# A new order of the pieces behind the first 47 in a hand-ordered attention and feed-forward kernel

## Chip, core and metric

The kernel runs on one core of a Trainium2 chip. The metric is the device time of one execution in microseconds (us), the median of the runs. The engines are TensorE (PE; its weight loads are shown as PEld), VectorE (DVE), ScalarE (ACT), GpSimd (POOL) and SyncE (SP), which here only issues transfers.

## What is computed

The reference normalizes x (2048 rows of 512), and adds to x an attention branch A and a feed-forward branch B of the same normalized rows. A has 32 heads of width 16 and walks four segments of 512 rows: causal softmax attention inside a segment, and a linear-attention memory M, z that is carried from one segment to the next and mixed in by a gate per head.

```python
for s in range(N):                      # N = 4 segments
    logits = einsum('bhqd,bhkd->bhqk', qs, ks) * scale + mask
    a_dot = einsum('bhqk,bhkd->bhqd', softmax(logits), vs)
    num = einsum('bhld,bhde->bhle', phi(qs), M)
    den = einsum('bhld,bhd->bhl', phi(qs), z)[..., None] + 1e-06
    outs.append(g * num / den + (1.0 - g) * a_dot)
    M = M + einsum('bhld,bhle->bhde', phi(ks), vs)
    z = z + einsum('bhld->bhd', phi(ks))
out = x + o @ wo + silu(xn @ w1) @ w2   # F = 1792
```

## The kernel before

The whole program is a list of words, ORDER, which is read from left to right; each word calls one small function (a piece), and that call issues its instructions. Every engine executes its own instructions in the order in which they were issued, so the list is the program order of all engines at once. There is no planner in the kernel: the list is written out. A word is a letter code, then the segment, then the tile, then sometimes a part, as in `k0.1.2`: key product, segment 0, tile 1, part 2. A tile is 128 of the 512 columns of q, k (eight heads), 128 rows of v and of the output, or 128 of the 1792 columns of h.

The words that matter here, with the line that their instructions carry in the profile:

- `S0` to `S71`, the scores: products of q and k in a shape of 32 rows (L701) into one tile psS of four PSUM banks, the exponential of all 2048 columns on ScalarE (L707, tile Pb), then two to four causal masks on GpSimd (L718, on Pb or into `lows`). S words are numbered 18 to a segment, nine to a pair of tiles; the list does not have them in the order of their numbers.
- `E`, `O`: the weights times v for the even and the odd heads of a tile (L763, psV), which need the masks of the S words of that tile. `Ev`, `Ov` or `Ea`, `Oa` copy the result out of PSUM on VectorE or ScalarE (L793, L800), and transfers move the sums of the softmax into `zraw` (L785). `Om` merges the odd heads by a predicated copy (L807).
- `k`, `q`, `v`, `h`: products with the weights (L331 as whole 128 x 128 products, L333 as four products 32 columns wide, which run side by side). `kv`, `qv`, `vv` copy them out of PSUM on VectorE, `ka`, `qa`, `va` on ScalarE (L373, L384, L391). A key copy also issues two masks of k on GpSimd (L376), which the scores read.
- `ha`, `hv`: tanh on ScalarE (L477) and the rest of the silu on VectorE (L482).
- `fp`, `fa`, `fv` and `gp`, `ga`, `gv`: phi of k and of q on GpSimd, ScalarE and VectorE (L402, L408, L418). `t` turns phi of k by a transfer (L426).
- `m`, `mv`, `mw`: the sums for the memory on TensorE (L437) and their additions and masks on VectorE. `s`, `sv`, `r`, `w`, `R`, `W`: the sums of the denominators, reciprocals, gate. `z`, `d` spread them by transfers (L562), `zv`, `dv` multiply (L574, L584), `n`, `nv` are the memory's product and its addition (L593).
- `o`, `oc`, `od`, `oh`: output products of a 512-, 256-, 128-column piece, and of half of the last tile; `st`, `sh` add the residual, which `xl` loads (L599), and store (L606, L611, L653, L657).
- `xs`, `xg`, `Nv`, `XD`: layer norm of the later segments (L281, L284, L292, L295, L310) and its turning by transfers (L829). `tb` loads the table for the exponential on ScalarE and runs one small exponential (L304). `lw` issues the loads of w2 and wo from ScalarE's queue.

The products other than the scores, and psV and psM, share four PSUM banks of 512 columns (`pp`, tag "pb"); a word that begins a product takes a free bank and waits for the copy that empties it. The last two output tiles use psS after the last scores.

```python
words = ORDER.split()
TILED = {"S": "rows", "E": "cols", "O": "cols", "s": "cols", "m": "cols", "X": "whole", "busy": "whole"}
...
    elif piece in ("k", "q", "v", "h", "n", "o", "oc", "od", "oh"):
        now = ahead[i] if now == "rows" else now
        now = "whole" if now == "rows" else now
    narrow[0] = now == "cols"
    PIECES[piece](*(int(n) for n in word[len(piece) :].split(".") if n))
```

So a product takes the shape of the words around it, and the shape changes around each S word.

Of the kernel before, what the change touches and what calls it, by code (L numbers as in the profile page):

```python
# [25 lines left out]
S6 vv1.0 v1.1.2 v1.1.3 xs10 lw0 xg8.4 h0.1.3 ha0.1 q1.2.0 t0.0 q1.2.1 q1.2.2 fv0.3 k1.2.0 vv1.1 k1.2.1 k1.2.2 k1.2.3 kv1.2
S8 q1.2.3 fa0.2 h0.2.0 h0.2.1 h0.2.2 h0.2.3 E1 qv1.2 gate hv0.1 h0.7.0
S9 q1.0.0 Ev1 fv0.2 t0.2 k1.1.0 k1.1.1 k1.1.2 Nv10 Nv11 h0.7.1 h0.7.2 h0.7.3 k1.1.3 kv1.1 ha0.7 hv0.7 q1.0.1 q1.0.2 Nv9 ha0.2 hv0.2
S10 h0.4.0 h0.4.1 XD10 t0.1 h0.4.2 h0.4.3 ha0.4 fp1.2 O1 Ov1 hv0.4 q1.0.3 h0.9.0 bmask qv1.0 gp1.0
S13 ga1.0 XD9 k1.3.0 h0.9.1 h0.9.2 k1.3.1 k1.3.2 xl0.2 h0.8.0 h0.8.1 xs13 h0.8.2 h0.8.3 k1.3.3 t0.3 kv1.3 ha0.8  # L30
# [11 lines left out]
S28 h1.4.0 h1.4.1 h1.4.2 q2.3.0 h1.4.3 ha1.4 q2.3.1 qv2.3 o0.0.9
S26 ga2.1 o0.0.1 oc0.0.13.0 od0.0.11.2 oc0.0.4.0 hv1.4 Nv12 O4 Ov4 q2.0.0 zv0.2 q2.0.1 qv2.0 zv0.0
S23 o0.0.2 XD12 h1.1.0 o0.0.16 h1.1.1 h1.1.2 od0.2.0.0 o0.2.16 h1.1.3 xl0.0 h1.12.0 ha1.1 od0.0.11.1 od0.0.11.0
S25 h1.12.1 h1.12.2 Om3 h1.12.3 od0.2.0.1 zv0.3 o0.0.14 oc0.0.4.1 hv1.1 gv1.1 o0.0.17 ha1.12 E5 Ev5 oc0.0.13.1
S29 o0.0.12 hv1.12 o0.0.8 od0.0.11.3 k2.3.0 zv0.1 k2.3.1 fa1.2 O5 kv2.3
S27 h1.6.0 mw0.0 fv1.2 o0.0.10 o0.0.6 t1.2 o0.0.5 gp2.1 h1.6.1 h1.6.2 o0.2.15 Ov5 h1.6.3 ha1.6 o0.0.0 hv1.6
# [5 lines left out]
S34 fp1.1 o0.1.0 v2.0.0 v2.0.1 vv2.0 h1.2.0 h1.2.1 fa2.3 o0.1.16 o0.3.17 Om6
S41 o0.3.8 o0.1.11 o0.1.1 O7 o0.1.14 oc0.1.12.1 fa1.1 o0.3.4 xl1.0 Ov7 o0.1.9
S37 o0.1.2 st0.1 h1.2.2 h1.2.3 o0.3.1 o0.3.3 o0.3.16 xl1.2 ha1.2 o1.2.4 od1.2.5.1 fv1.1 t1.1 m1.2 mv1.2 o1.2.1
S36 s1 hv1.2 o0.3.7 sv1 o0.3.2 fp2.0 r1.0 o0.3.14 st0.3 q3.1.0 q3.1.1 qv3.1 o1.2.12 fp2.3 fa2.0
S40 r1.1 v2.3.0 v2.3.1 vv2.3 h2.8.0 h2.8.1 r1.3 fv2.3 r1.2 ha2.8 hv2.8 q3.2.0
S43 q3.3.0 q3.3.1 qv3.3 w1 o1.2.8 q3.2.1 fa2.2 qv3.2 k3.1.0 d1.1 od1.2.5.2
# [24 lines left out]
S64 o2.0.13 od2.2.6.1 s3 sv3 o2.0.1 h3.12.0 h3.12.1 ha3.12 n2.1 r3.0 nv2.1 o2.2.0
S68 hv3.12 od2.0.7.2 o2.2.17 o2.0.11 h3.2.0 h3.2.1 o2.3.0 r3.2 r3.1 od2.3.9.3 o2.3.1 ha3.2 hv3.2 oc2.3.2.0
# [830 lines left out]
```

## Time and profile before

| what | value |
|---|---|
| median of 3 runs | 222.15 us (222.1 to 222.64) |
| profiled execution | 222.15 us; its span 220.4 us |
| TensorE busy, share of the span | 214.9 us, 97% |
| ScalarE | 184.0 us, 83% |
| VectorE | 179.7 us, 82% |
| GpSimd | 135.1 us, 61% |
| granted TensorE clock | 0.999 |
| S0 on TensorE, S71 on TensorE | 12.51 us, 193.15 us |

The span runs from the first to the last instruction. A timeline row gives the start, the duration, the engine, the line, the operation, output and inputs, shapes, a count where alike instructions stand in a row, and in brackets the idle time before it with what ended it. A group row gives count, busy time and mean duration in ns, then the idle time of the engine before such instructions. A windows row gives, for a stretch of time, busy time and count of each engine in the order PE, PEld, DVE, ACT, POOL, then the granted clock and the transfers' share and rate.

### The profile page before, as it was taken

To read this page: it belongs to the slowest core of one execution; us is meant where nothing else is said; L and a number is where in the kernel's file an instruction comes from. 1 tells how busy PE (TensorE), PEld (TensorE's weight loads), DVE (VectorE), ACT (ScalarE), POOL (GpSimd) and SP (SyncE) were. 2 spreads that over 40 slices of the span, in tenths; PEclk is the share of its full clock that TensorE was granted. 3 is DMA by queue.
4 is the path that set the end of the run, shared out by engine and by line. 5 is a ranking of instruction groups with operands and counts; after the bars stand their busy time and mean duration, and the time that the engine had idled before them with its cause. 6 is when DMAs were issued, how large, how long until landed. Compare 5 with 4: busy or idle time off the path is not lost.

```text
span 220.4 us, 9441 instructions
## 1 busy us (share of the span) xinstructions
PE 214.9 (97%) x4057; PEld 117.2 (53%) x4057; DVE 179.7 (82%) x368; ACT 184.0 (83%) x173; POOL 135.1 (61%) x253
## 2 busy tenths in 40 slices
PE   7999999999999999999999999999999999999994
PEld 7666645655553444454544444455454544455662
DVE  7789999988889788776897888969789887579554
ACT  3699999999999999999998999999989997971000
POOL 6089667997769976876669696693756364320000
PEclk9999999999999999999999999999999999999999
DMA  5993549552014221223303130142242020232313
GB/s 183 373 385 87 74 27 304 106 77 58 21 28 122 88 59 29 50 51 76 102 17 95 40 96 4 28 92 59 52 120 64 15 76 7 75 94 68 109 51 97
DMA packets 32746, 19.61 MB, mean 89 GB/s; under 512 B 14656, under 2 KB 32192, under 8 KB 32704
## 3 DMA queue, kind: packets, MB, share of 16 engines
q1 hardware_dynamic: 30080, 16.39, 28.6%
q10 hardware_dynamic: 2624, 2.62, 3.9%
q8 instruction: 31, 0.51, 1.0%
q14 instruction: 11, 0.09, 0.2%
HBM read 9.96 MB, written 2.10 MB: 55 GB/s over the span
## 4 chain that ended last, share of the span: by engine, by line
PE 79%; ACT 10%; DVE 4%; POOL 4%; issue 2%; POOLq 0%
PE ps L331 21%; PE psO L333 16%; PE ps L333 13%; PE psS L701 10%; PE psO L331 9%; ACT Pb L707 7%; PE psV L763 6%; PE psS L333 4%; POOL Pb L718 2%; DVE xn_t L310 1%; POOL lows L718 1%; ACT ex L408 1%; ACT th L477 1%; PE psM L437 1%; DVE stats L281 1%
## 5 line engine op out<-in xcount | busy, mean ns | idle before, releaser
L707 ACT ACTIVATE Pb<-psS 128x2048 bf16<-128x2048 f32 x72 | 135.2, 1878 | 7.5 <-PE psS L701 6.4
L718 POOL TENSOR_SCALAR_AFFINE_SELECT Pb<-Pb 128x256 bf16<-128x256 bf16 (+2 forms) x120 | 66.1, 571 | 22.3 <-ACT Pb L707 19.5
L482 DVE SCALAR_TENSOR_TENSOR hT<-th,ps 128x512 bf16<-128x512 bf16 x56 | 37.7, 679 | 9.1 <-ACT th L477 8.5
L718 POOL TENSOR_SCALAR_AFFINE_SELECT lows<-Pb 64x256 bf16<-64x256 bf16 (+1 forms) x56 | 26.7, 490 | 27.7 <-ACT Pb L707 25.3
L333 PE MATMUL psO<-w_sb,hT 128*32 128x512 bf16 (+2 forms) x716 | 42.5, 319 | 0.0
L331 PE MATMUL ps<-xnT,w_sb 128*128 128x512 bf16 (+1 forms) x160 | 35.2, 334 | 0.0
L477 ACT ACTIVATE th<-ps 128x512 bf16<-128x512 f32 x56 | 33.0, 598 | 2.2 <-PE ps L333 2.1
L333 PEld LDWEIGHTS <-hT 128*32 128x32 bf16 x884 | 21.8, 96 | 14.0 <-issue 3.3
L333 PE MATMUL ps<-xnT,w_sb 128*32 128x512 bf16 (+1 forms) x480 | 27.1, 341 | 0.1
L701 PE MATMUL psS<-qT,k 32*128 32x64 bf16 (+3 forms) x512 | 23.0, 233 | 0.8 <-ACT Pb L707 0.3
L331 PE MATMUL psO<-w_sb,hT 128*128 128x512 bf16 (+2 forms) x87 | 22.7, 334 | 0.0
L701 PEld LDWEIGHTS <-k 32*128 32x128 bf16 x512 | 9.8, 92 | 23.2 <-issue 21.7
L763 PE MATMUL psV<-Pb,Vz 128*32 128x448 bf16 (+7 forms) x512 | 21.6, 286 | 0.3 <-POOL Pb L718 0.3
L331 PEld LDWEIGHTS <-w_sb 128*128 128x128 bf16 x160 | 14.9, 98 | 12.1 <-issue 1.6
L763 PEld LDWEIGHTS <-Vz 128*32 128x32 bf16 x768 | 16.5, 97 | 9.1 <-issue 1.1
L376 POOL TENSOR_SCALAR k<-kT,pm_odd 128x512 bf16<-128x512 bf16 x16 | 12.0, 748 | 8.0 <-ACT kT L373 7.0
L333 PEld LDWEIGHTS <-w_sb 128*32 128x32 bf16 x480 | 11.9, 96 | 7.3 <-issue 1.9
L331 PE MATMUL ps<-wv_sb,xnT 128*128 128x512 bf16 x56 | 15.1, 381 | 0.2
L701 PE MATMUL psS<-qT,kT 16*128 16x448 bf16 (+3 forms) x256 | 14.7, 269 | 0.0
L333 PE MATMUL psO<-wo_sb,oT 128*32 128x512 bf16 x156 | 14.4, 380 | 0.0
L331 PE MATMUL ps<-xnT,wk_sb 128*128 128x256 bf16 (+1 forms) x64 | 13.6, 326 | 0.0
L793 DVE CAST oraw<-psV 128x512 bf16<-128x512 f32 x16 | 11.0, 689 | 3.0 <-PE psV L763 2.9
(110 smaller groups left out, 321.2 us busy)
## 6 DMA issues: line engine op xcount, KB each, us to landing
spr<-rz SPq DMA_DIRECT2D x56, 64.0 KB
x_res<-in_A_x_dram SPq DMA_DIRECT2D x16, 128.0 KB
out_dram<-o_out SPq DMA_DIRECT2D x15, 128.0 KB
w_sb<-in_B_w_dram SPq DMA_DIRECT2D x1, 1792.0 KB
w_sb<-in_B_w_dram ACTq DMA_DIRECT2D x1, 1792.0 KB
x_hi<-in_A_x_dram SPq DMA_DIRECT2D x2, 512.0 KB
wv_sb<-in_A_wv_dram SPq DMA_DIRECT2D x2, 256.0 KB
wk_sb<-in_A_wk_dram SPq DMA_DIRECT2D x1, 512.0 KB
```

The source lines that it names most:

```text
L281: nc.vector.bn_stats(out=stats[t][:], in_=xs(t, t + 1)[:, 0, :])
L310: eng.tensor_scalar(out=xn[t][:], in0=xs(t, t + 1)[:, 0, :], scalar1=mv_all[:, t, 0:1], scalar2=rstd_all[:, t, 0:1], op0=ALU.subtract, op1 ...
L331: return [nc.tensor.matmul(out, lhsT=lhsT, rhs=rhs, start=start, stop=stop, skip_group_check=True)]
L333: nc.tensor.matmul(out[c : c + 32], lhsT=lhsT[:, c : c + 32], rhs=rhs, start=start, stop=stop, tile_position=(0, c), skip_group_check=True,)
L376: nc.gpsimd.tensor_scalar(out=to, in0=frm, scalar1=keep[:, 0:1], scalar2=1.0, op0=ALU.mult, op1=ALU.mult)
L477: nc.scalar.activation(out=th[:], in_=sts[s]["h", ft][:, :], func=AF.Tanh, scale=0.5)
L482: nc.vector.scalar_tensor_tensor(out=st["hT"][:, ft, :], in0=st.pop(("th", ft))[:], scalar=1.0, in1=st.pop(("h", ft))[:, :], op0=ALU.add, ...
L701: nc.tensor.matmul(psS[:, g, c : c + q2 - q1], lhsT=keys[rows], rhs=st["qT"][rows, dt, q1:q2], start=True, stop=True, tile_position=(32 * ...
L707: exp = nc.scalar.activation(out=Pb[:, :, :], in_=psS[:, :, :], func=AF.Exp, scale=SCALE)
L718: over[id(Pb)].append(nc.gpsimd.affine_select(out=out, in_=in_, compare_op=ALU.is_ge, fill=0.0, base=base, pattern=[[0, out.shape[1]], [1, ...
L763: nc.tensor.matmul(psV[32 * g : 32 * g + 32, q0 : q0 + nq], lhsT=Vzs[s % 2][:, kt, 4 * dt + g, par : par + 2, :].rearrange("p a d -> p (a ...
L793: copy(out=oraw[:], in_=sts[s].pop(("psV", 0))[:, :])
```

## The change

Only ORDER changes. Its first 47 words stay (through `k0.0.1`); the 1286 behind them are in a new order. Both lists have 1333 words. Nine words differ in kind: `qv0.0`, `kv0.1`, `vv2.3`, `Ev14`, `Ev15`, `Oa12` and `Oa14` become `qa0.0`, `ka0.1`, `va2.3`, `Ea14`, `Ea15`, `Ov12` and `Ov14`, and `qa0.1` and `qa3.0` become `qv0.1` and `qv3.0`. The order of the S words among themselves is the same. It is said of the new list that it was searched with the predicated copy at its measured length, and under late small transfers and fetches of instructions.

Behind `k0.0.1` the first line continues:

```diff
-k0.1.0 k0.0.2 k0.0.3 k0.3.0 q0.0.0 q0.0.1 q0.0.2 q0.0.3 ka0.0 fp0.0 qv0.0 tb fa0.0 q0.2.0 k0.1.1 k0.1.2 k0.1.3 kv0.1 fp0.1
+tb xs6 k0.1.0 k0.1.1 k0.0.2 k0.0.3 ka0.0 k0.1.2 fa0.0 q0.0.0 q0.0.1 q0.0.2 q0.0.3 qa0.0 k0.1.3 q0.3.0 q0.3.1 k0.3.0 ka0.1 fp0.1
```

and some whole lines of the list are

```diff
-S0 q0.1.0 q0.1.1 q0.1.2 q0.1.3 k0.3.1 xs4 xs6 xs7 xs5 xg4.4 q0.2.1 q0.2.2 qa0.1 q0.2.3 qv0.2
...
-S1 Nv5 vv0.2 h0.5.0 h0.10.0 h0.10.1 h0.10.2 v0.3.3 vv0.3 xs8 Nv6 XD6 h0.5.1 h0.5.2 XD5 h0.5.3 ha0.5
-S3 q0.3.0 q0.3.1 q0.3.2 q0.3.3 hv0.5 k0.2.0 qv0.3 Nv4 XD4 k0.2.1 k0.2.2 tanh h0.10.3 ha0.10
...
-S15 hv0.12 hv0.9 h1.11.1 h1.11.2 h1.11.3 ha1.11 E2 Ev2 O2 h1.9.0 h1.9.1
...
-S20 z0.2 k2.0.0 hv1.8 z0.1 h1.5.2 h1.5.3 z0.3 gp1.1 k2.0.1 kv2.0 E4 Ev4 ha1.5 hv1.5 od0.2.0.3
...
-S35 od0.1.8.3 o0.1.13 oc0.3.13.0 o0.3.5 o0.3.12 o0.1.7 E7 Ev7 xl0.1 od0.3.10.0 ga1.3 oc0.1.12.0 o0.3.9 gv1.3 fp1.0 fv1.0 t1.0
...
+S0 xs4 k0.3.1 q0.2.0 q0.2.1 xs5 k0.3.2 xs7 v0.2.0 v0.2.1 xg4.4 k0.3.3 fa0.1 q0.3.2 q0.3.3
...
+S1 Nv5 XD5 h0.11.0 hv0.5 fv0.1 h0.11.1 h0.11.2 h0.10.0 h0.10.1 q0.1.1 q0.1.2 h0.11.3 ha0.11 h0.10.2
+S3 Nv4 hv0.11 h0.10.3 ha0.10 q0.1.3 qv0.1 v0.3.0 v0.3.1 v0.3.2 fp0.3 h0.13.0 Nv7 XD7 h0.13.1 h0.13.2 v0.3.3 vv0.3 xs11
...
+S15 E2 Ev2 q1.3.2 q1.3.3 qv1.3 h1.11.1 h1.11.2 gp1.1 h1.11.3 ha1.11 xs12 xs14 xg12.4 o0.2.4
+S17 h1.9.0 h1.9.1 h1.9.2 h1.9.3 ha1.9 h0.0.0 h0.0.1 hv1.11 o0.2.10 XD11 o0.2.1 hv1.9 oc0.2.9.1
+S21 o0.2.12 O2 oc0.2.2.1 oc0.2.9.0 h0.0.2 m0.2 mv0.2 h0.0.3 Ov2 ha0.0 Om2 o0.2.5
...
+S20 k2.0.0 z0.0 h1.5.3 ha1.5 hv1.8 z0.2 z0.3 k2.0.1 kv2.0 oc0.2.2.0 o0.2.7 E4 Ev4 XD14
...
+S34 od0.1.8.2 fv1.3 o0.1.14 t1.3 Om5 o0.1.5 fp1.1 h1.2.0 h1.2.1 h1.2.2 h1.2.3 ha1.2 gv2.1 hv1.2 E7 oc0.3.13.1
```

The last line, behind `S71`, holds the rest of the output products of both lists; it ends in `st3.2` with eight `oh` words and `sh1` in the old list, and in `st3.0` with eight `oh` words and `sh0` in the new one.

More of the change, by code (lines that the diff above doesn't have):

```diff
@@ L26 @@
[L26 to L30, printed above, removed]
@@ L42 @@
[L42 to L47, printed above, removed]
@@ L53 @@
[L53 to L58, printed above, removed]
@@ new lines @@
+kind odd omask ones0 ones1 zeros xc0 xd0 xc1 xq0 xi0 Nv0 busy44 xd1 xq1 xc2 xi1 X0.1 Nv1 xd2 Xa0.1 busy6 v0.0.0 v0.0.1 xq2 X1.1 Xa1.1 xs3 v0.0.2 v0.0.3 xq3 v0.1.0 xi2 v0.1.1 v0.1.2 v0.1.3 Nv2 xi3 X2.1 va0.0 va0.1 Nv3 Xv2.1 X3.1 Xv3.1 k0.0.0 k0.0.1 tb xs6 k0.1.0 k0.1.1 k0.0.2 k0.0.3 ka0.0 k0.1.2 fa0.0 q0.0.0 q0.0.1 q0.0.2 q0.0.3 qa0.0 k0.1.3 q0.3.0 q0.3.1 k0.3.0 ka0.1 fp0.1
+S0 xs4 k0.3.1 q0.2.0 q0.2.1 xs5 k0.3.2 xs7 v0.2.0 v0.2.1 xg4.4 k0.3.3 fa0.1 q0.3.2 q0.3.3
+S2 kv0.3 qv0.3 q0.2.2 q0.2.3 qv0.2 v0.2.2 v0.2.3 vv0.2 q0.1.0 Nv6 h0.5.0 h0.5.1 XD6 h0.5.2 h0.5.3 ha0.5
@@ new lines @@
+S6 h0.2.0 h0.2.1 h0.2.2 Ov0 qv1.0 ga1.1 v1.0.0 fp0.2 v1.0.1 xs13 v1.0.2 v1.0.3 vv1.3 Nv8 XD8 k1.2.0 k1.2.1
+S8 h0.7.0 h0.7.1 Nv10 vv1.0 Nv11 h0.7.2 h0.7.3 h0.2.3 k1.2.2 k1.2.3 kv1.2 ha0.2 hv0.2 ha0.7 hv0.7 E1
+S9 h0.4.0 h0.4.1 h0.4.2 k1.0.0 k1.0.1 h0.4.3 k1.0.2 ha0.4 fv0.0 t0.0 Ev1 O1 Ov1 hv0.4
+S10 Om0 Nv9 XD9 k1.0.3 kv1.0 t0.3 h0.8.0 h0.8.1 h0.8.2 h0.8.3 XD10 q1.2.0 q1.2.1 q1.2.2 q1.2.3 qv1.2 fa0.2 ha0.8 hv0.8
+S13 xs15 h0.9.0 fv0.2 t0.2 k1.1.0 h0.9.1 h0.9.2 h0.9.3 k1.1.1 k1.1.2 k1.1.3 k1.3.0 k1.3.1 ha0.9
@@ new lines @@
+S12 h0.12.0 h0.12.1 h0.12.2 h0.12.3 t0.1 kv1.1 k1.3.2 k1.3.3 hv0.9 q1.3.0 ha0.12 kv1.3 q1.3.1 gate h1.11.0 hv0.12
+S15 E2 Ev2 q1.3.2 q1.3.3 qv1.3 h1.11.1 h1.11.2 gp1.1 h1.11.3 ha1.11 xs12 xs14 xg12.4 o0.2.4
+S17 h1.9.0 h1.9.1 h1.9.2 h1.9.3 ha1.9 h0.0.0 h0.0.1 hv1.11 o0.2.10 XD11 o0.2.1 hv1.9 oc0.2.9.1
+S21 o0.2.12 O2 oc0.2.2.1 oc0.2.9.0 h0.0.2 m0.2 mv0.2 h0.0.3 Ov2 ha0.0 Om2 o0.2.5
+S14 h1.10.0 h1.10.1 h1.10.2 h1.10.3 ha1.10 hv0.0 h0.3.0 h0.3.1 h0.3.2 h0.3.3 gv1.1 m0.0 mv0.0
+S16 hv1.10 od0.2.0.1 lw1 q2.1.0 Om1 q2.1.1 qv2.1 od0.2.0.3 E3 ha0.3 Ev3 o0.2.11 od0.2.0.2 hv0.3 o0.2.13 Nv13
@@ new lines @@
+S19 h0.6.0 h0.6.1 O3 Ov3 h0.6.2 h1.0.0 h0.6.3 ha0.6 h1.0.1 h1.0.2 hv0.6 Nv14
+S24 h1.0.3 k2.2.0 k2.2.1 kv2.2 ha1.0 gp1.0 v2.1.0 v2.1.1 bmask
+S18 o0.2.3 vv2.1 o0.2.8 hv1.0 sv0 v2.2.0 r0.3 r0.0 r0.1 v2.2.1 vv2.2 h1.8.0 ga1.0 h1.8.1 o0.2.6 xl0.2
+S22 h1.8.2 h1.8.3 ha1.8 k2.1.0 r0.2 k2.1.1 h1.5.0 h1.5.1 h1.5.2 kv2.1 w0 z0.1
+S20 k2.0.0 z0.0 h1.5.3 ha1.5 hv1.8 z0.2 z0.3 k2.0.1 kv2.0 oc0.2.2.0 o0.2.7 E4 Ev4 XD14
+S28 xl0.3 hv1.5 q2.3.0 q2.3.1 qv2.3 XD13 h1.4.0 h1.4.1 h1.4.2 h1.4.3 ha1.4 o0.0.9 od0.0.11.3
@@ new lines @@
+S26 q2.0.0 q2.0.1 hv1.4 o0.0.1 zv0.0 fa1.0 qv2.0 O4 Ov4 fp1.3 o0.0.8 oc0.0.4.0
+S23 h1.1.0 oc0.0.13.0 oc0.0.13.1 o0.0.3 Om3 zv0.3 h1.1.1 o0.0.2 h1.1.2 gv1.0 zv0.2 h1.1.3 ha1.1 o0.0.6 hv1.1 gp1.2 h1.12.0
+S25 zv0.1 h1.12.1 h1.12.2 h1.12.3 xl0.0 o0.0.5 o0.0.10 od0.2.0.0 E5 Ev5 o0.0.14 od0.0.11.2 ha1.12
+S29 o0.2.16 hv1.12 ga1.2 o0.0.15 k2.3.0 od0.0.11.1 Nv12 k2.3.1 O5 kv2.3
+S27 h1.13.0 h1.13.1 o0.2.14 Ov5 o0.2.15 gv1.2 o0.2.17 st0.2 h1.13.2 h1.13.3 xl0.1 ha1.13 hv1.13 fp1.0 o0.3.0 od0.3.10.0 od0.3.10.1 od0.3.10.2 fv1.0 oc0.3.11.1
```

95 lines of the change are left out of this document (45 added, 50 removed).

## The prediction

> **What bounds the kernel now.** I read the page first, then the view of waits, then the timeline of TensorE and ScalarE stage by stage; a stage is what lies between two score pieces (S words of the list). The last-ending chain is TensorE's own order nearly throughout, so the question is when TensorE stands still.
>
> ```profile
> PE 214.9 (97%) x4057; PEld 117.2 (53%) x4057; DVE 179.7 (82%) x368; ACT 184.0 (83%) x173; POOL 135.1 (61%) x253
> ```
> ```profile
> PEld L701 <- issue: 21.7, 64, 0.4
> ACT Pb L707 <- PE psS L701: 6.4, 18, 0.7
> PE psV L763 <- POOL Pb L718: 0.3, 1, 0.3
> ```
>
> TensorE waits for other engines hardly anywhere in this view, but that is deceptive: a matmul held back while the one before it drains counts as busy. So I take the distance from score piece to score piece, here the stage of S40 on TensorE:
>
> ```profile
> 108.59 0.21 PE L701 MATMUL psS<-qT,k 32*128 32x64 bf16 x4
> ...
> 108.93 1.04 PE L331 MATMUL ps<-wv_sb,xnT 128*128 128x512 bf16 x4
> 109.80 1.03 PE L331 MATMUL ps<-xnT,w_sb 128*128 128x512 bf16 x4
> 110.66 0.59 PE L331 MATMUL ps<-xnT,wq_sb 128*128 128x512 bf16 x2
> 111.19 0.40 PE L701 MATMUL psS<-qT,k 32*128 32x64 bf16 x8
> ```
>
> Ten products of 512 columns take the stage from 108.59 to 111.19, 2.60 us. Starts 108.93 and 109.80 are four products apart: 0.217 us each, which I call a unit (0.215 below, rounded). The score piece and the change of tile shape around it take the rest, 0.45 us. A stage of u units thus wants 0.45 + 0.215 u. Now a stage with eight units, the one of S3, on TensorE (256-column products, two to a unit) and on ScalarE:
>
> ```profile
> 19.81 0.40 PE L701 MATMUL psS<-qT,k 32*128 32x192 bf16 x8
> 20.14 1.05 PE L331 MATMUL ps<-xnT,wq_sb 128*128 128x256 bf16 x8
> 21.03 0.82 PE L331 MATMUL ps<-xnT,wk_sb 128*128 128x256 bf16 x6
> 21.68 0.38 PE L331 MATMUL ps<-xnT,w_sb 128*128 128x256 bf16 x2
> 22.19 0.21 PE L701 MATMUL psS<-qT,k 32*128 32x64 bf16 x4
> ```
> ```profile
> 17.88 1.88 ACT L707 ACTIVATE Pb<-psS 128x2048 bf16<-128x2048 f32 x1
> ...
> 20.26 1.88 ACT L707 ACTIVATE Pb<-psS 128x2048 bf16<-128x2048 f32 x1
> ...
> 22.64 1.88 ACT L707 ACTIVATE Pb<-psS 128x2048 bf16<-128x2048 f32 x1
> ```
>
> By its units it wants 0.45 + 1.72 = 2.17 us, and it takes 2.38 (19.81 to 22.19), the distance of the exponentials (20.26 to 22.64). There is one score tile in PSUM, so S4 waits for the exponential of S3 (ends 22.14), takes 0.40, and the next exponential starts 0.05 later. That loop is a floor of 2.38 us, or nine units: a stage with fewer loses the difference. So the time is the start of S0, plus 71 stages each the larger of units and floor, plus waits for VectorE and GpSimd, plus the products left behind S71.
>
> ```profile
> 12.51 0.21 PE L701 MATMUL psS<-qT,k 32*128 32x64 bf16 x4
> ...
> 193.15 0.40 PE L701 MATMUL psS<-qT,k 32*128 32x192 bf16 x8
> ...
> 217.16 0.40 PE L333 MATMUL psS<-wo_sb,oT 128*32 128x256 bf16 x8
> ```
>
> S0 stands at 12.51, S71 at 193.15 (71 stages, 180.64 us), the last product ends at 217.56, and the span of 220.4 us leaves 2.87 behind it for the last half tile's addition and store. The profiled execution took 222.15 us, 1.7 outside its span, and is the median of the three times. A difference of 0.3% (0.67 us) is about what a measurement of this kernel can tell from none.
>
> **The change, part by part.** Counted from the lists: both have 1333 words and the same 72 score pieces, so the shape changes cost the same; TensorE has the same products. What moves is which stage a product fills, five PSUM copies between VectorE and ScalarE, and how far a consumer stands behind its producer.
>
> *Start, about +0.4 us.* The exponential table's load (tb) moves ahead of the first key copy (ka0.0); the query copy of tile 0 and the key copy of tile 1 go to ScalarE, ahead of S0's exponential.
>
> ```profile
> 8.93 0.59 ACT L391 CAST Vz<-ps 128x512 bf16<-128x512 f32 x1 [0.19 <-PE ps L331]
> 9.21 1.57 PE L331 MATMUL ps<-xnT,wk_sb 128*128 128x256 bf16 x12
> 10.60 0.59 ACT L373 CAST kT<-ps 128x512 bf16<-128x512 f32 x1 [1.08 <-PE ps L331]
> 11.20 1.28 ACT L304 ACT_TABLE_LOAD   x1
> 12.50 0.20 ACT L304 ACTIVATE spare<-eps 128x1 f32<-128x1 f32 x1
> ```
>
> Before, ScalarE idles from 9.52 to 10.60 and loads behind the copy. After, load and first exponential run 9.52 to about 11.0, so ka0.0 ends at 11.6 instead of 11.19; S0 stood 1.32 behind it (GpSimd's two masks of k), so S0 comes at 12.9: +0.4. The added copies end about when S0's exponential may start. The list now has 15 units between the first key product and S0 instead of 14; by 3.3/14 us each (9.21 to 12.51) these would let S0 start at 12.75, so the bounds are +0.2 and +0.6 (both copies in the way).
>
> *Units moved, -0.55 and +0.3.* From S0 to S71 the old list has 666.75 units, the new 664.25: 2.5 x 0.215 = 0.54 less. Behind S71 there are 111.75 instead of 110.25: 1.5 x 0.215 = 0.32 more. The one unit of difference is the one that now lies before S0.
>
> *Stages below the floor, -0.8.* A sums product of the memory (m) in a stage counts as one unit. The old list has four stages of 8 units (S0, S1, S3, S7), four of 8.5 (S8, S10, S17, S24) and six of 8.75 (S16, S20, S26, S23, S25, S29): 4 x 0.21 + 4 x 0.10 + 6 x 0.05 = 1.54 us lost. The new one has one of 8 (S5), five of 8.5 (S7, S11, S15, S17, S21) and one of 8.75 (S29): 0.76. That is 0.78 less.
>
> *Stages with two small ScalarE pieces, -0.1.* Such a stage has a floor of its own, here the one of S9:
>
> ```profile
> 37.29 1.88 ACT L707 ACTIVATE Pb<-psS 128x2048 bf16<-128x2048 f32 x1
> ...
> 39.06 1.08 ACT L477 ACTIVATE th<-ps 128x512 bf16<-128x512 f32 x2
> ...
> 40.02 1.90 ACT L707 ACTIVATE Pb<-psS 128x2048 bf16<-128x2048 f32 x1
> ```
>
> 2.73 us, the worth of 10.6 units. Twelve become nine; TensorE is often past that anyway, so I take 0.1 and no bound beyond 0.3.
>
> *Waits, -0.45.* Two stages ran long because of GpSimd's masks:
>
> ```profile
> 47.39 0.10 PEld L701 LDWEIGHTS <-k 32*128 32x128 bf16 x4 [0.42 <-issue]
> ...
> 49.58 0.40 PE L763 MATMUL psV<-Pb,Vz 128*32 128x320 bf16 x8 [0.26 <-POOL Pb L718]
> ...
> 50.47 0.40 PE L701 MATMUL psS<-qT,k 32*128 32x192 bf16 x8
> ```
> ```profile
> 96.28 0.40 PE L701 MATMUL psS<-qT,k 32*128 32x192 bf16 x8
> ...
> 96.92 0.44 DVE L807 COPY_PREDICATED oraw<-omask,odd 128x256 int32<-128x256 int32 x1
> 96.96 0.87 POOL L718 TENSOR_SCALAR_AFFINE_SELECT Pb<-Pb 128x512 bf16<-128x512 bf16 x1
> ...
> 98.92 0.40 PE L701 MATMUL psS<-qT,k 32*128 32x64 bf16 x8
> ```
> ```profile
> L718 POOL TENSOR_SCALAR_AFFINE_SELECT Pb<-Pb 128x512 bf16<-128x512 bf16 x48 | 30.9, 661 | 2.2
> ```
>
> S15's stage has ten units (2.60) and takes 3.08: O2 stands one stage behind S12, whose masks are late. S35's has nine (2.38) and takes 2.64: E7 waits for a mask that took 0.87 instead of 0.66, beside a predicated copy. The new list puts O2 two stages later (in S21) and E7 one stage later (end of S34). That takes away 0.48 + 0.26 = 0.74, but it moves other weighings closer (E2 now opens the second stage behind its last mask, and E4 stands 0.3 us earlier behind its own); I keep 0.3 for one new wait of the smaller size. Bounds: -0.74 if none is new, +0.5 if two of O2's size come.
>
> The Trainium skill, SBUF — State Buffer, section "SBUF: two separate sides", says that VectorE with two SBUF inputs and GpSimd share a port pair by an exclusive lock, so that whoever starts second stands still for the whole instruction. The trace agrees, here by 0.21 us (0.87 against 0.66). If each of the two new neighbours of a weighing met such a lock, the sum would be 0.4 higher; without the rule it is the one below.
>
> *Sum:* +0.4 - 0.54 + 0.32 - 0.78 - 0.1 - 0.45 = -1.15 us; 222.15 - 1.15 = 221.0. The end stays as it is: eight half products and one half store behind the last whole tile in both lists, 2.87 us.
>
> **The rivals.** *(1) VectorE falls behind between S0 and S17, slower.*
>
> ```profile
> 12.51:50.47 37.96, 36.97 (x595) 22.11 (x596) 35.48 (x72) 37.33 (x36) 31.54 (x58) 1.00 0.63 140
> ```
> ```profile
> L384 DVE CAST qT<-ps 128x512 bf16<-128x512 f32 x14 | 9.6, 683 | 2.7 <-PE ps L331 2.7
> L281 DVE BATCH_NORM_STATS2 stats<-x_hi 128x6 f32<-128x512 bf16 x8 | 5.4, 673 | 0.0
> L284 DVE BATCH_NORM_AGGREGATE mv_all<-stats 128x2 f32<-128x6 f32 x16 | 2.9, 181 | 0.5
> ```
>
> VectorE (third figure) is busy 35.48 of that stretch's 37.96. The new list puts two more query copies (2 x 0.68) and two more layer-norm sums (2 x 0.85) into it and takes one copy of 0.2 out: +2.86, 38.34 us. If the stretch stays at 37.9 and VectorE idles its old 2.48 in it, it ends 2.9 late, and each late copy holds one of the four PSUM banks that the products share. Against it: the first two sums can run before S0, while VectorE has nothing else (1.7 us of lead), and products wait only once a copy is later than the banks allow. It decides when the lead is lost (VectorE then waits for k0.3's product until S0's stage is over) and the banks cover no more than half a microsecond: then 2.4 reach TensorE, and the time is 223.4.
>
> *(2) The waits come back in other places.* Three waits of the sizes seen (0.48, 0.26 and the 0.21 by which that mask was late) beside the one kept: 221.0 + 0.95 = about 222.0, no change. For it: VectorE, GpSimd and ScalarE all run within a tenth of the stage, so a piece shifted by a few tenths finds no slack.
>
> *(3) The list does not do what it says,* because the floor is not lost where I count it and the copies moved to ScalarE push exponentials back: without the floor's 0.78 the sum is -0.37, 221.8, no change.
>
> **How the numbers follow.** The forecast, about 221.0, has a chance of 0.55; its own range is 220.2 (start +0.2, no new wait, 0.2 more at two-piece stages) to 221.4 (start +0.6, one wait of O2's size more). Rival (2) gets 0.18, rival (3) 0.08, rival (1) 0.19. Range 220.2 to 223.2: above lies part of rival (1), below little. Faster 0.55, same 0.26, slower 0.19.
>
> **What would show it.** Right: S0 near 12.9, the table load at 9.5; S71 near 191.6 (from 12.9 less than 179.0 for 71 stages); the stages of S1 and S3 on nine units at 2.38 with TensorE nowhere short; O2 and E7 without a mask just ended before them; 24.7 us from S71 to the last product. Wrong: products between S9 and S17 that start just as a VectorE copy ends (rival 1), stages of S15, S20, S34 longer than their units because a mask ends late (rival 2), or a start of S0 past 13.3.

## The result: slightly slower

The changed kernel takes 223.07 us (median; 222.44 to 223.84), the kernel before in the same comparison 222.50 (222.07 to 223.66). The ratio is 1.0027, 95% interval 1.0017 to 1.0036: 0.57 us slower, where 221.0 and thus 1.15 us faster was forecast. A second comparison gave 222.94 against 222.32, ratio 1.0031 (1.0016 to 1.0046).

The first profiled execution of the changed kernel took 223.32 us, 0.25 above its median, so a second one (222.78 us) stands beside it. Each span, cut at the places that the prediction used (us):

| kernel | S0 | S0 to S71 | S71 to end of last product | from there to the end | span |
|---|---|---|---|---|---|
| before | 12.51 | 180.64 | 24.41 | 2.87 | 220.4 |
| forecast | 12.9 | 178.8 | 24.7 | 2.87 | 219.3 |
| after | 12.88 | 179.84 | 25.37 | 3.52 | 221.6 |
| after, second profile | 12.82 | 179.93 | 24.73 | 3.49 | 221.0 |

The second profile against before: +0.31 - 0.71 + 0.32 + 0.62 = +0.54 us, which is close to the 0.57 of the medians. The start and the tail's products came as forecast; the stages won 0.7 to 0.8 instead of 1.87; the end, forecast at nothing, lost 0.62.

### The profile page after: what moved, and what is told of

It reads as the page before. It is cut to its first block, busy times and chain, and to the rows that moved or that the text cites. A ratio compares the mean times of both kernels' runs of the same rounds, so it can differ in the third digit from the quotient of the medians.

```text
span 221.6 us, 9593 instructions
## 1 busy us (share of the span) xinstructions
PE 215.4 (97%) x4129; PEld 117.4 (53%) x4129; DVE 179.1 (81%) x367; ACT 185.1 (84%) x174; POOL 136.2 (61%) x253
## 3 DMA queue, kind: packets, MB, share of 16 engines
q1 hardware_dynamic: 30080, 16.39, 27.6%
q10 hardware_dynamic: 2624, 2.62, 3.7%
## 4 chain that ended last, share of the span: by engine, by line
PE 73%; ACT 7%; POOL 6%; DVE 4%; DMA 3%; issue 3%; SPq 2%; DVEq 0%; POOLq 0%
PE ps L331 19%; PE ps L333 14%; PE psO L333 13%; PE psS L701 9%; PE psV L763 7%; PE psO L331 6%; ACT Pb L707 5%; POOL Pb L718 2%; PE psS L836 2%; SPq L562 2%; DMA spr<-rz 2%; POOL k L376 1%; PE psS L333 1%; POOL lows L718 1%; POOL pos L402 1%
## 5 line engine op out<-in xcount | busy, mean ns | idle before, releaser
L718 POOL TENSOR_SCALAR_AFFINE_SELECT Pb<-Pb 128x256 bf16<-128x256 bf16 (+2 forms) x120 | 67.4, 582 | 22.3 <-ACT Pb L707 19.3
L333 PE MATMUL psO<-w_sb,hT 128*32 128x512 bf16 (+2 forms) x744 | 46.5, 323 | 0.0
L331 PE MATMUL ps<-xnT,w_sb 128*128 128x512 bf16 (+1 forms) x156 | 33.2, 332 | 0.1
L333 PE MATMUL ps<-xnT,w_sb 128*32 128x512 bf16 (+1 forms) x496 | 28.1, 344 | 0.0
L331 PEld LDWEIGHTS <-w_sb 128*128 128x128 bf16 x156 | 14.1, 97 | 11.7 <-issue 2.8
L331 PE MATMUL psO<-w_sb,hT 128*128 128x512 bf16 (+2 forms) x80 | 19.3, 327 | 0.1
L333 PEld LDWEIGHTS <-w_sb 128*32 128x32 bf16 x496 | 12.5, 96 | 7.9 <-issue 1.4
L331 PE MATMUL ps<-wv_sb,xnT 128*128 128x512 bf16 x49 | 13.4, 380 | 0.2
L606 DVE SCALAR_TENSOR_TENSOR o_out<-psO,x_res 128x512 bf16<-128x512 f32 x14 | 9.6, 686 | 3.9 <-PE psO L333 2.2
L800 DVE CAST odd<-psV 128x512 bf16<-128x512 f32 x15 | 10.3, 685 | 2.5 <-PE psV L763 2.4
```

Source lines behind the costliest of these rows:

```text
L331: return [nc.tensor.matmul(out, lhsT=lhsT, rhs=rhs, start=start, stop=stop, skip_group_check=True)]
L333: nc.tensor.matmul(out[c : c + 32], lhsT=lhsT[:, c : c + 32], rhs=rhs, start=start, stop=stop, tile_position=(0, c), skip_group_check=True,)
L606: out = nc.vector.scalar_tensor_tensor(out=o_out[:], in0=st.pop(("psO", j)), scalar=0.5, in1=st["x", j][:], op0=ALU.mult, op1=ALU.add)
L718: over[id(Pb)].append(nc.gpsimd.affine_select(out=out, in_=in_, compare_op=ALU.is_ge, fill=0.0, base=base, pattern=[[0, out.shape[1]], [1, ...
L800: copy(out=odd[:], in_=sts[s].pop(("psV", 1))[:, :])
```

## The profile after

The page of the changed kernel, engines and the chain that ended last:

```profile
PE 215.4 (97%) x4129; PEld 117.4 (53%) x4129; DVE 179.1 (81%) x367; ACT 185.1 (84%) x174; POOL 136.2 (61%) x253
...
PE 73%; ACT 7%; POOL 6%; DVE 4%; DMA 3%; issue 3%; SPq 2%; DVEq 0%; POOLq 0%
```

New against before is what stands in the chain beside TensorE: transfers and SyncE's queue, 5% between them. The timeline of the start (ScalarE, then TensorE) and the two score pieces that answer to those quoted before:

```profile
9.59 1.28 ACT L304 ACT_TABLE_LOAD   x1
...
10.99 0.57 ACT L373 CAST kT<-ps 128x512 bf16<-128x512 f32 x1
...
12.88 0.21 PE L701 MATMUL psS<-qT,k 32*128 32x64 bf16 x4 [0.18 <-POOL k L376]
...
192.72 0.40 PE L701 MATMUL psS<-qT,k 32*128 32x192 bf16 x8
```

The table load at 9.59, the key copy to 11.56 and S0 at 12.88 are the forecast's 9.5, 11.6 and 12.9. The two waits that were to go are gone. The stage of S15, now 8.5 units, takes 2.39 (47.38 to 49.77 on TensorE; it was 3.08 with ten units, which want 2.60); the stage of S21, where O2 now stands, takes 2.37 (52.15 to 54.52); that of S35 takes 2.43 (was 2.64).

```profile
47.38 0.21 PE L701 MATMUL psS<-qT,k 32*128 32x64 bf16 x4
...
49.77 0.40 PE L701 MATMUL psS<-qT,k 32*128 32x192 bf16 x8
...
52.15 0.40 PE L701 MATMUL psS<-qT,k 32*128 32x192 bf16 x8
...
54.52 0.21 PE L701 MATMUL psS<-qT,k 32*128 32x64 bf16 x4
```

Others came. The largest three, on the timelines of TensorE, GpSimd and VectorE:

```profile
69.25 0.40 PE L701 MATMUL psS<-qT,k 32*128 32x64 bf16 x8
...
70.99 1.04 PE L763 MATMUL psV<-Pb,Vz 128*32 128x512 bf16 x16
71.96 0.21 PE L701 MATMUL psS<-qT,k 32*128 32x64 bf16 x4
```
```profile
67.99 0.61 POOL L402 TENSOR_SCALAR pos<-qT 128x512 bf16<-128x512 bf16 x1
...
70.59 1.09 POOL L718 TENSOR_SCALAR_AFFINE_SELECT Pb<-Pb 128x1024 bf16<-128x1024 bf16 x1
```
```profile
88.96 0.89 DVE L807 COPY_PREDICATED oraw<-omask,odd 128x256 int32<-128x256 int32 x1
```
```profile
139.81 1.02 PE L331 MATMUL ps<-xnT,wk_sb 128*128 128x512 bf16 x4 [0.19 <-DVE oT L593]
```

In the stage of S20, nine units, E4 takes 1.04 us instead of some 0.72 (what it takes in the last experiment): it stands for the mask that ends at 71.68, which GpSimd reaches late behind the piece of gp1.0 (67.99). The stage takes 2.72 instead of 2.38. In that of S30 (2.62) a predicated copy of 0.89 us (0.44 where it is alone) makes the silu behind it late, whose PSUM bank the next product needs. In that of S51 (2.85, ten units want 2.60) the product k3.3 waits for a bank until the memory's addition (L593) has read it.

And the end, on VectorE and the last product on TensorE:

```profile
211.65 0.42 DVE L574 TENSOR_TENSOR oT<-spr,oraw 128x512 bf16<-128x512 bf16 x1 [1.20 <-DMA spr<-rz]
...
216.19 0.69 DVE L606 SCALAR_TENSOR_TENSOR o_out<-psS,x_res 128x512 bf16<-128x512 f32 x1 [0.82 <-PE psS L333]
216.84 0.42 DVE L653 SCALAR_TENSOR_TENSOR o_half<-psS,x_res 128x256 bf16<-128x256 f32 x1
217.80 0.69 DVE L606 SCALAR_TENSOR_TENSOR o_out<-psO,x_res 128x512 bf16<-128x512 f32 x1 [0.54 <-DMA out_dram<-o_out]
218.78 0.42 DVE L653 SCALAR_TENSOR_TENSOR o_half<-psS,x_res 128x256 bf16<-128x256 f32 x1 [0.28 <-DMA out_dram<-o_out]
```
```profile
212.92 0.29 PE L333 MATMUL psS<-wo_sb,oT 128*32 128x256 bf16 x4 [0.46 <-DVE oT L593]
...
217.81 0.28 PE L333 MATMUL psS<-w_sb,hT 128*32 128x256 bf16 x4
```

The row tiles and the half tiles share three buffers (name "o_out", bufs=3). The new list adds and stores its last five tiles between 214.7 and 219.2, and the last two additions wait, not for TensorE, but for stores issued three before them to land: that is the 3.52 us behind the last product. The row at 211.65 is another matter: the transfer z3.3 lands late and oh17.1 stands at 212.92; in the second profile of the same kernel it does not (below).

## The experiments

Two theories. **E and F**: the loss lies at the end (buffers, E), and in transfers whose last share is held up by a fetch of instructions (F; the page lists 32 of them on a queue of their own, 0.52 MB, so 16 KB each); the stage waits (W) add. **The rivals (N)**: removing any of these only moves the wait. All ratios are to the kernel before, run beside.

**The half stores in other buffers.**

```diff
- o_half = work.tile([P, D], BF16, name="o_half", tag="o_out", bufs=3)[:, 0 : D // 2]
+ o_half = work.tile([P, D], BF16, name="odd")[:, 0 : D // 2]
```

> The changed kernel with one line altered: the two half stores write from the tile "odd" (two buffers, long read out by then) and no longer share the three buffers of the row stores. Nothing of the list is altered. Theory E (the end waits for buffers): sh1, st3.0 and sh0 no longer wait for stores issued three before; last product to end goes back from 3.52 to about 2.9 us, and the kernel takes 0.6 us less, 222.5 against 223.1, level with the kernel before (ratio to it 1.000). Rival N (the end is limited by landing the last stores, whichever buffer they leave from): last product to end stays at 3.4 to 3.5 us and the time at 223.1 (ratio 1.0027).

Measured: 222.33 us, ratio 1.0003 (0.9987 to 1.0019). VectorE's end, and the last product (ends 217.55):

```profile
216.73 0.69 DVE L606 SCALAR_TENSOR_TENSOR o_out<-psO,x_res 128x512 bf16<-128x512 f32 x1
217.60 0.42 DVE L653 SCALAR_TENSOR_TENSOR odd<-psS,x_res 128x256 bf16<-128x256 f32 x1 [0.18 <-PE psS L333]
```

Last product to end is 2.89 again. Theory E holds, and this one line is worth the whole of the net loss: the kernel before, run beside, took 222.34.

**The tail's stall covered.** oh17.1, o3.2.17, o3.1.17 and st3.1 some nine words later.

```diff
- ... o3.0.0 oh17.1 xl3.2 oh10.1 o3.1.1 st2.1 oc3.1.0.1 o3.2.17 oc3.1.9.1 xl3.0 o3.0.8 o3.0.1 o3.1.17 oh7.1 st3.1 o3.0.4 ...
+ ... o3.0.0 xl3.2 oh10.1 o3.1.1 st2.1 oc3.1.0.1 oc3.1.9.1 xl3.0 o3.0.8 o3.0.1 oh7.1 o3.0.4 oh17.1 o3.2.17 o3.1.17 st3.1 ...
```

> The changed kernel with oh17.1, o3.2.17, o3.1.17 and st3.1 moved some nine words back in the tail, behind products that do not need the last spread transfer. Theory Z (TensorE stands 0.64 us at oh17.1 for the transfer z3.3, whose last ring lands 2 us after the others): the 1.3 us of products in front cover it, the stall at oh17.1 falls under 0.1 us, S71 to last product from 25.4 to 24.8 us, and the time by 0.6 us to about 222.5. Rival N (the stall only moves: the other row products wait in turn, or st3.1 later pushes the end back): S71 to last product falls by under 0.2 us, or last product to end rises by as much as is won, and the time stays at 223.0 or over. If the buffers at the end are what bounds it, up to 0.3 us of the gain can be lost there.

Measured: 222.93 us, 1.0039 (1.0025 to 1.0054): no gain. S71 to the last product is 24.73, but it is 24.81 in the run above too, which has the stall's words in their old places. So there was nothing to cover in a usual execution. The run shows something else, on TensorE in the stage of S2:

```profile
17.36 1.05 PE L331 MATMUL ps<-xnT,w_sb 128*128 128x256 bf16 x8 [0.66 <-DMA w_sb<-in_B_w_dram]
```

The first product with w_sb stands for the load of w_sb, which lands at 17.32, and S2 takes 3.23 us.

**Three stage waits worked round.** gp1.0 goes behind hv1.5 in S28, n1.1 and nv1.1 go to S50, and Om4 goes ahead of fv1.0.

```diff
- ... ha1.0 gp1.0 v2.1.0 ...
+ ... ha1.0 v2.1.0 ...
- S51 Ev10 k3.3.0 k3.3.1 mw1.2 o1.2.17 h2.1.0 h2.1.1 kv3.3 n1.1 ha2.1 nv1.1
+ S51 Ev10 o1.2.17 mw1.2 o1.2.14 k3.3.0 k3.3.1 h2.1.0 h2.1.1 kv3.3 ha2.1
- ... o0.3.3 Om4 ha1.6
+ ... o0.3.3 ha1.6
```

> The changed kernel with three of its new stage waits worked round and nothing else: gp1.0 goes from S24 to S28, so that GpSimd reaches the masks that E4 reads 0.6 us sooner; in S51 k3.3 goes behind o1.2.17 and o1.2.14 (n1.1 goes to S50), so that its bank is free; the predicated copy Om4 goes into VectorE's idle time before fv1.0. Theory W (waits add up): the stages S20, S30 and S51 fall from 2.72, 2.62 and 2.85 to about 2.42, 2.40 and 2.60, together 0.7 us less, and the time goes to about 222.4 (ratio to the kernel before 0.9995). Rival N (a stage's wait comes back in the next stage, at ScalarE's 2.38 us or at another mask): S0 to S71 falls by under 0.3 us and the time stays at 222.8 to 223.1. Om4 beside GpSimd's multiplication should take 0.6 to 0.9 us, 0.44 if it is alone.

Measured: 224.09 us, 1.0078 (1.0057 to 1.0098). The three stages fell as expected (2.39, 2.38, 2.64), and two others rose by more. One is the experiment's own fault: with n1.1 in S50, o1.1.15 waits 1.2 us for its addition (S50 3.83). The other is this, on VectorE and TensorE:

```profile
79.37 0.43 DVE L574 TENSOR_TENSOR oT<-spr,oraw 128x512 bf16<-128x512 bf16 x1 [1.18 <-DMA spr<-rz]
```
```profile
82.03 0.73 PE L763 MATMUL psV<-Pb,Vz 128*32 128x512 bf16 x16 [0.84 <-DVE hT L482]
```

By the trace's transfer records, seven of the eight shares of z0.3 landed by 77.59 and the eighth at 79.24; a fetch of 1.21 us had begun at 76.51. VectorE stood in its order, the silu behind it was late, and S25 took 3.42.

**The fetches moved.**

```diff
- ... busy44 ...
+ ... busy20 ...
```

> The changed kernel with 20 instead of 44 of the warm-up products at the start (busy20 for busy44): 24 products and 24 weight loads less in TensorE's stream, so that every later fetch of instructions, one for each 256 instructions, comes about 1.0 us later (the one at 208.59 near 209.6). Theory F (this fetch holds up one ring of the transfer z3.3): the last ring of z3.3 lands near 209.6 and not 211.55, the 0.64 us stall at oh17.1 is gone, and the time is 0.6 us less, about 222.5, if the start keeps its pace. Rival N (the transfer is late by its own queue): the last ring lands near 211.5 again, with the fetch elsewhere. A third way: fewer warm-up products lower the granted clock at the start, S0 comes over 0.2 us later than 12.88, and this hides the gain; S0 and the clock of the first slices tell.

Measured: 224.42 us, 1.0105 (1.0084 to 1.0125). The start lost its pace; TensorE's timeline here, and then the same six products in the changed kernel:

```profile
1.10 2.31 PE L836 MATMUL psS<-zraw 128*128 128x128 bf16 x20 [1.10 <-DVE zraw L183]
...
7.93 2.77 PE L331 MATMUL ps<-wv_sb,xnT 128*128 128x512 bf16 x6
...
14.62 0.21 PE L701 MATMUL psS<-qT,k 32*128 32x64 bf16 x4
```
```profile
7.28 1.67 PE L331 MATMUL ps<-wv_sb,xnT 128*128 128x512 bf16 x6
```

Six products that take 1.67 us in the changed kernel take 2.77 here, and S0 comes 1.74 us later. The granted clock of this run, 0.999, does not show it. The Trainium skill, TensorE: Matmul & The Clock Gate, Part 1, has TensorE at half rate until some 3.4 us of sustained work. With 2.31 us of warm-up products the trace agrees. Beside that, the fetches moved: the first came at 18.2, the load of w_sb landed by 16.24 with its last two shares 0.23 apart, and S2 took 2.40, though here the first product with w_sb came only at 18.44.

**The fetches moved at equal warm-up.** One product of 256 columns for each two of 128.

```diff
- nc.tensor.matmul(idle[:, 0:P], lhsT=zraw[:, 0:P], rhs=zraw[:, 0:P], start=True, stop=True)
+ nc.tensor.matmul(idle[:, 0 : 2 * P], lhsT=zraw[:, 0:P], rhs=zraw[:, 0 : 2 * P], start=True, stop=True)
- ... busy44 ... busy6 ...
+ ... busy22 ... busy3 ...
```

> The changed kernel with each two warm-up products of 128 columns made one of 256 (22 and 3 for 44 and 6): the same work and the same time on TensorE with some 50 instructions fewer, so every fetch of its instructions comes about 1 us later and the first one, at 13.4 to 13.8 us in the runs so far, comes near 16. Theory F (that fetch delays the last share of the load of w_sb, for which the product h0.5.0 of stage S2 stands waiting): w_sb lands by 16.3 instead of 16.7 to 17.5, the stage S2 takes 2.40 instead of 2.49 to 3.33, the transfer z3.3 is not met by a fetch, and the time is 0.3 to 0.6 us less than 223.07 (ratio to the kernel before 1.000 to 1.0015). Rival N (the load is late by its own bytes): w_sb lands at 16.7 to 17.5 as before, S2 keeps its 2.5 to 3.3, and the ratio stays at 1.0027.

Measured: 223.48 us, 1.0052 (1.0037 to 1.0068). At the front theory F holds: the first fetch came at 16.6 and w_sb landed at 15.92. The load of w_sb in eight of the profiles (us; share: one of the parts in which a transfer lands):

| profile | first fetch | last share but one | last share | first product with w_sb | S2's stage |
|---|---|---|---|---|---|
| before | 13.7 | 15.78 | 16.89 | 17.76 (in S1) | 2.39 |
| after | 13.7 | 15.92 | 16.74 | 16.79 | 2.49 |
| after, second | 13.8 | 16.39 | 16.93 | 16.98 | 2.74 |
| half stores | 13.4 | 15.69 | 16.93 | 16.97 | 2.84 |
| tail covered | 13.6 | 16.04 | 17.32 | 17.36 | 3.23 |
| three waits | 13.8 | 16.41 | 17.49 | 17.54 | 3.33 |
| waits again | 14.0 | 16.55 | 16.74 | 17.11 | 2.40 |
| wide warm-up | 16.6 | 15.85 | 15.92 | 16.54 | 2.40 |

In the next experiment (waits again) the share is late too, but there S0 came at 13.29 and the product asked later. In the six profiles whose first fetch came at 16.0 or later, the load landed between 15.89 and 16.36.

But the last fetch moved as well: at 215.2 it began 0.6 us behind the issue (214.56) of a store of the end, not at or ahead of it as in the two profiles of the changed kernel. That store landed at 217.87, and the end, still with its three buffers, took 4.32 us:

```profile
217.99 0.69 DVE L606 SCALAR_TENSOR_TENSOR o_out<-psO,x_res 128x512 bf16<-128x512 f32 x1 [1.56 <-DMA out_dram<-o_out]
```

So the gain at the front was eaten at the end, as a run below shows by taking the end out.

**The stage waits again, n1.1 left in its place.**

> The changed kernel with three stage waits worked round as in the third run, but with n1.1 and nv1.1 left where they were (there they made o1.1.15 wait 1.2 us): gp1.0 in S28, Om4 ahead of fv1.0, k3.3 of S51 behind o1.2.17 and o1.2.14. Theory W: S20, S30 and S51 with S50 lose 0.3, 0.23 and 0.3 us, and the time is 0.7 us less than the changed kernel's 223.07 (ratio to the kernel before 0.9995). If the fetch at 76.5 again meets the transfer z0.3, S25 takes 3.4 us and eats 1.0 us: then the ratio is near 1.004 (theory F). Rival N (waits only move): S0 to S71 falls by under 0.3 us without any fetch on an awaited transfer.

Measured: 222.69 us, 1.0022 (1.0004 to 1.0041). Its stages of S20 and S30 take 2.39 and 2.38, but S25 takes 2.68 instead of 2.39, and S51 2.94 with one more product in it. No fetch had a part in that. Why S25, is seen in the next run, which has the same words there.

**All of these together.**

> The changed kernel with the half stores in buffers of their own, the wide warm-up products and the three stage waits worked round. If the three losses are apart from each other, they add up: 0.6 (end) and 0.3 to 0.6 (w_sb) and 0.7 (stages) less than 223.07, about 221.3 (ratio to the kernel before 0.995). If they hide one another, 222.0 to 222.4 (ratio 0.999).

Measured: 221.85 us, 0.9974 (0.9962 to 0.9986), faster than both kernels. From 223.07 that is 1.2 us of the 1.8 that adding up gives. S25, on GpSimd, TensorE and VectorE, then the same multiplication in the changed kernel:

```profile
78.36 1.02 POOL L402 TENSOR_SCALAR pos<-kT 128x512 bf16<-128x512 bf16 x1
...
80.01 0.63 POOL L718 TENSOR_SCALAR_AFFINE_SELECT Pb<-Pb 128x512 bf16<-128x512 bf16 x1
```
```profile
80.69 0.73 PE L763 MATMUL psV<-Pb,Vz 128*32 128x512 bf16 x16
```
```profile
78.84 0.82 DVE L574 TENSOR_TENSOR oT<-spr,oraw 128x512 bf16<-128x512 bf16 x1
```
```profile
79.13 0.41 DVE L574 TENSOR_TENSOR oT<-spr,oraw 128x512 bf16<-128x512 bf16 x1
```

The piece taken away from in front of E4's mask pushes GpSimd's later pieces back. They now stand beside VectorE's work on two SBUF tiles, and each is the longer for it: GpSimd's piece at 78.36 takes 1.02 instead of 0.67, VectorE's multiplication 0.82 instead of 0.41. TensorE pays on GpSimd's side: E5 starts at 80.69 because the mask that it reads ends at 80.64, 1.70 us into the stage and not 1.34 as in the changed kernel. The silu before E5 ended at 80.27, in time. The Trainium skill, SBUF — State Buffer, section "SBUF: two separate sides", has GpSimd, and VectorE with two SBUF inputs, share a port pair under an exclusive lock. The trace agrees with it.

**The wide warm-up in the kernel before.**

> The kernel before with the wide warm-up products alone. There the first product with w_sb comes 0.4 us after its landing and no stage waits for it. Theory F: the time stays within 0.2 us of 222.4, unless a later fetch now meets an awaited transfer. Rival (the wide products themselves warm TensorE better or start S0 sooner): S0 moves by over 0.1 us and the time with it, and then the gain of the changed kernel with them is no proof for the fetch.

Measured: 222.15 us, 0.9993 (0.9985 to 1.0002). S0 moves by 0.11 (12.40), the first product with w_sb had 0.87 us to spare there (17.76 against 16.89), and the time does not move measurably. In the changed kernel, too, the wide products do not bring S0 forward: it comes at 12.71 to 13.29 with the old ones and at 12.72 to 13.12 with the wide ones. So the gain there is not one of warmth.

**The changed kernel once more.**

> The changed kernel itself, once more, to see which of its losses are there in every execution. Theory E with F (in the median: the end costs 0.65, stage S2 waits 0.1 to 0.9 for w_sb, and the stall at z3.3 was one execution's): last product to end 3.5 us again, S2 over 2.45, S71 to last product 24.7 to 24.9 and no stall at oh17.1, ratio to the kernel before 1.0027. Rival (the stall at z3.3 belongs to the list): S71 to last product 25.3 us again with over 0.5 us at oh17.1.

Measured: 222.94 us, 1.0031 (1.0016 to 1.0046). Its profile has S2 at 2.74, 3.49 us at the end, and no stall at oh17.1 (TensorE, then VectorE):

```profile
212.32 0.28 PE L333 MATMUL psS<-wo_sb,oT 128*32 128x256 bf16 x4
```
```profile
217.04 0.69 DVE L606 SCALAR_TENSOR_TENSOR o_out<-psO,x_res 128x512 bf16<-128x512 f32 x1 [0.39 <-DMA out_dram<-o_out]
218.14 0.42 DVE L653 SCALAR_TENSOR_TENSOR o_half<-psS,x_res 128x256 bf16<-128x256 f32 x1 [0.41 <-DMA out_dram<-o_out]
```

The end's wait belongs to the list; the 0.64 us at z3.3 belonged to one execution.

**Half stores and wide warm-up, the list of the stages as changed.**

> The changed kernel with the wide warm-up products and the half stores in buffers of their own, its list of the stages untouched. Theory F with E: the gain at S2 (0.1 to 0.9 us), which the end ate in the run with the wide products alone, now shows: 0.3 to 0.5 us less than the run with the half stores alone (222.33), about 221.9, ratio to the kernel before 0.998. Rival N (S2 is not worth its time, because S71's products wait for later work anyway): 222.2 to 222.4, ratio 1.000.

Measured: 222.03 us, 0.9984 (0.9968 to 1.0001); S2 2.40, end 2.89. That is 0.3 less than with the half stores alone (222.33); the intervals of the two overlap, so the size of S2's share is read from the stages, 0.1 to 0.9 by execution, and not from this difference.

**Two of the stage repairs done otherwise.** gp1.0 at the end of S20, behind E4; in S51 only o1.2.17 ahead of k3.3; Om4, half stores and warm-up as above.

> As the kernel with all repairs (221.85), with two of its stage repairs done otherwise: gp1.0 stands at the end of S20, behind E4 but ahead of the masks of S28 on GpSimd (there it ran at 76.6 beside VectorE's z3 multiplications, which then took 0.82 instead of 0.41 us, and S25 took 2.68 instead of 2.39), and S51 takes only o1.2.17 ahead of k3.3, not o1.2.14 too. If what was lost in S25 was the port shared by GpSimd and VectorE, S25 is back at 2.40 with S20 at 2.40, S51 at 2.75, and the time 0.3 to 0.4 us less, 221.5 (ratio 0.996). Rival: GpSimd's 0.6 us comes out wherever it stands, in S28 or S26 instead, and the time stays at 221.8 to 221.9.

Measured: 221.54 us (221.43 to 221.8), 0.9964 (0.9951 to 0.9977), the fastest of all, span 219.7. E4 no longer stands (TensorE):

```profile
68.98 0.40 PE L701 MATMUL psS<-qT,k 32*128 32x64 bf16 x8
...
70.72 0.72 PE L763 MATMUL psV<-Pb,Vz 128*32 128x512 bf16 x16
71.37 0.21 PE L701 MATMUL psS<-qT,k 32*128 32x64 bf16 x4
```

S51 is at 2.72 as expected, but S52 behind it rose from 2.54 to 2.75, and S25 stays at 2.63: there the rival was right, GpSimd's 0.6 us comes out wherever it stands (E5 again starts, at 80.29, as its mask ends, at 80.25). S0 to S71 is 179.38, in the kernel with all repairs 179.32. So the time came out as expected, and not for the reason given: the two profiles differ at S0 (12.72 against 13.12) and at the end (2.90 against 3.27), places where no word was changed. The intervals of the two overlap, so that their medians truly differ by 0.3 is not shown, and why they would stays open.

## Why the prediction was wrong, by its own steps

- *Start, +0.4.* Right: S0 at 12.88 and 12.82, for the reason given (table load, copy, masks).
- *Units, floors, two-piece stages, -1.42 together.* Right as far as the stages tell. The larger of 0.45 + 0.215 u and the floors, added over 71 stages, is 179.35 for the old list and 177.95 for the new one, 1.40 less; that is the rule's own working. In the stages themselves, S1, S3, S7, S17 and S24 of the old list, with 8 and 8.5 units, take 2.38 or 2.39, where their units want 2.17 to 2.28, and S6, S12 and S40, ten units before and nine after, fall from 2.61 to 2.39 or 2.40. Of the two stages named as signs, S3 came at 2.39, S1 at 2.52.
- *Units behind S71, +0.32.* Right: 24.73 against 24.41 in the second profile.
- *Waits, -0.45.* This step failed. Above the rule the old list stands 1.3 us (180.64 - 179.35), the new one 1.9 to 2.0 (179.84 and 179.93 - 177.95): +0.6 to +0.7 instead of -0.45. The two waits named went, 0.74 in all, and O2 and E7 were placed as argued. What was mis-sized is the term for new ones: one of 0.3 was kept, and there came 0.34 (S20, E4, the very weighing the text named), 0.25 (S51), 0.24 (S30), 0.1 to 0.9 (S2, w_sb), and seven or eight of 0.12 to 0.18 (S1, S13, S16, S36, S39, S49 and S52 in both profiles, S9 in the second): some 2.0 in the first profile, 2.3 in the second. More had gone, too, than was named: S10, S19 and S0 of the old list stood 0.26, 0.25 and 0.15 above the rule and came down to it. That leaves +0.6 to +0.9, near what was measured. The term's upper bound, +0.5, was passed.
- *The end stays as it is.* This step failed by itself: 2.87 became 3.5. I compared the products and stores behind the last whole tile, and not how closely the last five stores follow one another with three buffers. The trace of the old list had the numbers for it: the store issued at 215.41 lands at 217.12, 0.49 before the addition three places later (217.61) wants its buffer. In the new list the store that counts is issued at 216.91, lands at 218.66 (1.75 us, with no late share), and the addition follows at 218.78. With the half stores in other buffers the like store lands at 218.10, and the addition stands at 217.60, 0.50 ahead of it. The first of the two waits at the end holds a late share of a store in both profiles, but the second sets the end.
- *Rival (2), the waits come back,* was the mechanism; it was priced at 222.0, without the end. *Rival (1)* did not happen, and its working was too high: VectorE was busy for 35.01 of the 36.89 us between S0 and S17 of the changed kernel, not for 38.34 (the row below the list). Two of the layer-norm sums began at 11.40 and 12.23, ahead of S0, though VectorE had stood for the load of x_hi until then; one key copy and one copy of odd heads also left that stretch. VectorE waited 0.25 us for k0.3's product, not to the end of S0's stage. The place of this rival was taken by a load: the new list asks for w_sb 1.1 us sooner (16.67 where it does not wait, with the half stores and the wide warm-up, against 17.76). *Rival (3)* does not fit the stages named above, which stand on the floor where it was counted.
- The prediction's own range was not added up rightly: one more wait of O2's size and a start of +0.6 come to 221.7, not 221.4.
- The late z3.3 of the first profile would have been a fine story for 0.64 us. A second profile of the same kernel and the run that covered it say that it is no part of the median.

```profile
12.88:49.77 36.89, 36.59 (x604) 21.90 (x605) 35.01 (x72) 35.76 (x33) 31.16 (x55) 1.00 0.54 136
```

Left open: why S1, S13, S16, S36, S39, S49 and S52 stand 0.12 to 0.18 above the rule was not tried one by one.

## What to carry to other kernels

A sum over stages prices what each engine has to do; it doesn't price how closely a consumer follows its producer, and that is what a search over orders tightens everywhere at once: count the pairs that moved closer, buffers and loads among them, instead of allowing for one wait. At the end of a kernel compare, for each of the last stores, its landing with the addition that takes the same buffer next. Take a second profile before explaining a stall of one execution, above all behind a transfer.

## What the hardware showed that was not expected

**Fetches of instructions hold up transfers.** TensorE's stream is fetched while it runs, in pieces of 16 KB: some 50 of its instructions fewer moved the first fetch from 13.4 to 14.0 us in the runs with the old warm-up to 16.0 to 17.2. Of the spreading transfers (L562, eight shares each) in thirteen profiles, 718 with all shares on record, 37 had a last share over 0.6 us behind the one before it, mostly 1.3 to 2.2. In every one of the 37 a fetch had begun between 0.5 us before the issue and the landing of the seventh share; of the others, 244 also had such a fetch and took no harm. Which transfer is hit depends on how many instructions precede it and on tenths of a microsecond of the execution, so a waiting consumer should have 2 us of cover, or the fetch should be moved by lengthening or merging instructions ahead of it, as the wide warm-up did.

**A predicated copy waits out what GpSimd has begun.** In the thirteen profiles there are 208 of them. The 119 that began with no piece of GpSimd running (or, twice, beside one on a tile of 128 x 4) took 0.43 to 0.46 us, also where GpSimd began one after them. The 89 that began while a piece was running took 0.43 to 0.89: three of them met the last 0.06 us of a piece and lost nothing, and the others ended 0.29 to 0.32 us behind the end of that piece. The copy of 0.89 us at 88.96 met this mask (it ends at 89.55, the copy at 89.85):

```profile
88.88 0.67 POOL L718 TENSOR_SCALAR_AFFINE_SELECT lows<-Pb 64x512 bf16<-64x512 bf16 x1 [0.58 <-ACT Pb L707]
```

So the price is what is left of the piece: where the third experiment moved the copy and 0.6 to 0.9 was expected, it met the last 0.18 us of a mask and took 0.48.
